# Tokens of a 128-block in another order, longer load runs, sinks over SP: a change to a sliding-window attention and SwiGLU kernel

## The chip, the cores and the metric

The kernel runs on one core of a Trainium2 chip. A core has five engines that run beside each other, each through its own queue in order: TensorE (PE, matrix products and transposes), VectorE (DVE), ScalarE (ACT), GpSimd (POOL) and SyncE (SP). Here POOL and SP mostly issue DMAs; 16 DMA engines do the moving. SBUF is the working memory (128 partitions), PSUM the small memory into which PE writes and which DVE and ACT must empty. The metric is the time of one execution in microseconds; lower is better.

## What is computed

Attention of 4 batches, 8 heads, 768 tokens and head size 64, in which a token sees the 128 latest tokens and the first 4 of its batch (the sinks), then a gated feed-forward block over all 3072 tokens:

```python
scores = scale * np.matmul(q, k.transpose(0, 1, 3, 2))
is_sink = pos[None, :] < int(n_sink)              # 4
rel = pos[:, None] - pos[None, :]
in_window = (rel >= 0) & (rel < int(window))      # 128
scores = np.where(is_sink | in_window, scores, -1000000000.0)
a = softmax(scores); attn = np.matmul(a, v)       # [4, 8, 768, 64]
x = attn.transpose(0, 2, 1, 3).reshape(3072, 512)
g = x @ w_gate                                    # 512 x 1536
out = (g * sigmoid(g)) * (x @ w_val) @ w_out      # [3072, 512]
```

Inputs and output are float32 in HBM; the kernel works in bfloat16 and sums in float32. Loads from POOL's queue convert on the way, so 256 bytes read of a row are 128 bytes written.

## The kernel before

A *group* is 256 tokens (12 groups, 3 per batch), a *block* is 512 tokens of the feed-forward part (6 blocks). Attention of a group runs in steps. **T** (`step_T`): for a pair of heads, four PE transposes turn K and Q into `kqT` (channels on partitions); one copy of 128x512 takes them from PSUM, on ACT, or on DVE for half of them at the start. **S** (`step_S`): scores of a pair of heads into the PSUM tile `s`, ACT takes the exponential into `e`, DVE multiplies by a mask. **K** (`step_K`): scores against the sinks, `es`. **PV** (`step_PV`): per 128 tokens and four heads, nine products of `e` with V (`va`, with a column of ones) and of `es` with the sinks' V (`vsb`); DVE divides. **X** (`step_X`): four transposes give `xT`, the input of the feed-forward block. A block is 12 *gate* units (products `pg` and `pv`, ACT's tanh `th`, DVE's `u` and `ht`) and 4 *down* units (12 products `pd`, ACT's copy `ot`, an output DMA by SP).

The order is written by hand. `later` holds DVE work that is issued a step afterwards (`flush`). First groups 0 and 1 run alone (lines 389 to 394, here called the start); then, in the loop at line 395, the attention steps of the next two groups are put between the two halves of the gates (a table `slots`). DVE's work for a gate frees PSUM: pool `ps_f` has three buffers, and a gate's `pg` is free when `u` is done, its `pv` when `ht` is done. T, K and X share one PSUM buffer (`ps_t`), PV has two (`ps_o`).

All loads stand on POOL's queue in the order of the program: K and Q of groups 0 and 1 with their V, masks, gate weights, group 2, the output weights, group 3, and then the sinks `vc`, 32 DMAs of four rows (line 185). A DMA that POOL issues waits for the one eight before it. The sinks are spread over the heads by one DVE product per batch, `vsb` (line 223), issued in `step_ks` when the batch's first T steps are done. The loads of later groups follow when T of an earlier group is through (line 319).

Of the kernel before, what the change touches and what calls it, by code (L numbers as in the profile page):

```python
# [15 lines left out]
def kernel(  # L16
# [26 lines left out]
    TB = 512  # L43
    NTB = NTOK // TB
    VS = 72
    FG = 3
# [17 lines left out]
    xtp = pool("xtp", 2)  # L64
# [6 lines left out]
    ps_o = pool("ps_o", 2, True)  # L71
    ps_t = pool("ps_t", 1, True)
# [6 lines left out]
    def load_group(g, split=1):  # L79
        b, c = divmod(g, GC)  # L80
        t0 = c * 256
        kq = natp.tile([P, 2, 2, H * D], BF16, tag="kq", name="kq")
        va = vpool.tile([P, 2, H, VS], BF16, tag=f"va{g}", name="va")
        hn = H // split
        for s in range(split):
            hs = slice(s * hn, (s + 1) * hn)
            for i, src in ((0, k), (1, q)):
                for j in range(2):
                    nc.gpsimd.dma_start(  # L89
                        kq[:, i, j, s * hn * D:(s + 1) * hn * D].rearrange(  # L90
                            "p (h d) -> p h d", d=D),
                        src[b, hs, t0 + j * P:t0 + (j + 1) * P].rearrange(
                            "h p d -> p h d"),
                    )
        for j in range(2):
            nc.gpsimd.dma_start(  # L96
                va[:, j, :, 0:D],
                v[b, :, t0 + j * P:t0 + (j + 1) * P].rearrange("h p d -> p h d"),
            )
        nat[g], vas[g] = kq, va  # L100
# [3 lines left out]
    def load_gate(i):  # L104
        n = FG * P
        for lst, w, nm in ((wgs, moe_w_gate, "wg"), (wvs, moe_w_val, "wv")):
            t = wpool.tile([P, DMC, n], BF16, tag=f"{nm}{i}", name=nm)
            nc.gpsimd.dma_start(
                t, w[:, i * n:(i + 1) * n].rearrange("(c p) f -> p c f", p=P))
            lst.append(t)  # L110
# [14 lines left out]
    vcs, vsbs, kss = [], [], []  # L125

    load_group(0, split=2)
    make_identity(nc, ident)


    def build_mask(m, sink):
        nc.gpsimd.memset(m, 1.0)
        for j in range(2):
            pv_, dg = m[:, j, 0:P], m[:, j, P:2 * P]
            nc.gpsimd.affine_select(
                out=pv_, in_=pv_, compare_op=ALU.is_gt, fill=0.0, base=0,
                pattern=[[-1, P]], channel_multiplier=1)
            if sink:
                nc.gpsimd.affine_select(
                    out=pv_, in_=pv_, compare_op=ALU.is_ge, fill=1.0, base=-NS,  # L140
                    pattern=[[0, P]], channel_multiplier=1)
            nc.gpsimd.affine_select(
                out=dg, in_=dg, compare_op=ALU.is_ge, fill=0.0, base=0,
                pattern=[[1, P]], channel_multiplier=-1)
            if sink and j == 0:

                nc.gpsimd.affine_select(
                    out=dg, in_=dg, compare_op=ALU.is_ge, fill=1.0, base=-NS,
                    pattern=[[0, P]], channel_multiplier=1)

    load_group(1)
    build_mask(mask0, True)
    load_gate(0)
    load_gate(1)
    build_mask(mask, False)
    load_gate(2)
    load_gate(3)
    load_group(2)


# [6 lines left out]
        pattern=[[NS, H]], channel_multiplier=-1)  # L167
    KS = P + 2 * NS
    for b in range(B):
        vc = const.tile([P, D + 1], BF16, tag=f"vc{b}", name="vc")  # L170
        nc.vector.memset(vc, 0.0)
        nc.vector.memset(vc[:, D:D + 1], 1.0)
        ks = const.tile([P, NP2 * KS], BF16, tag=f"ks{b}", name="ks")
        nc.vector.memset(ks, 0.0)
        vsb = const.tile([P, H, D + 1], BF16, tag=f"vsb{b}", name="vsb")
        vcs.append(vc)
        kss.append(ks)
        vsbs.append(vsb)

    for i in range(4):  # L180
        load_out(i)
    load_group(3)
    for b in range(B):
        for h in range(H):
            nc.gpsimd.dma_start(vcs[b][h * NS:(h + 1) * NS, 0:D], v[b, h, 0:NS])

    def ones_v(g):
        nc.vector.memset(vas[g][:, :, :, D:D + 1], 1.0)
# [10 lines left out]
    def step_T(g, p, on_dve=False):  # L199
        b, c = divmod(g, GC)  # L200
        if c == 0 and p == 0:
            kqT[b] = kqtp.tile([P, NP2, 2, S], BF16, tag="kqT", name="kqT")
        pt = ps_t.tile([P, 2, 2, P], BF16, tag="pt", name="pt")
        for i in range(2):
            for t in range(2):
                nc.tensor.transpose(  # L206
                    pt[:, i, t], nat[g][:, i, t, p * P:(p + 1) * P], ident)
        dst = kqT[b][:, p, :, c * 256:(c + 1) * 256].rearrange(
            "q i (t r) -> q i t r", t=2)
        if on_dve:  # L210
            nc.vector.tensor_copy(out=dst, in_=pt)  # L211
        else:
            nc.scalar.copy(out=dst, in_=pt)  # L213

    def step_ks(g):

        b = g // GC
        dst = kss[b].rearrange("q (a m) -> q a m", m=KS)
        for h in range(2):
            r = slice(h * D, (h + 1) * D)  # L220
            nc.vector.tensor_copy(
                out=dst[r, :, h * NS:(h + 1) * NS], in_=kqT[b][r, :, 0, 0:NS])
        nc.vector.tensor_tensor(  # L223
# [86 lines left out]
    def T(g, p):  # L310
        def f(pro=False):
            if p == 0:
                ones_v(g)
# [135 lines left out]
```

## Time and profile before

| | us |
|---|---|
| median of 3 runs (327.3 to 330.65) | 330.06 |
| the profiled run / its span | 327.02 / 325.2 |
| start, to the first gate | 0 to 74.4 |
| block 0, with attention of groups 2 and 3 | 74.4 to 117.55 |
| blocks 1 to 4, 43.74, 42.51, 42.99 and 43.75 | to 290.54 |
| block 5, without attention, and the end | to 325.2 |

All numbers are of one profiled execution. Busy times of engines overlap, so they don't add up to the span; what counts is which wait ends last in a stretch. Mean durations of PE rows hold pipelining: products of one kind start closer together than each lasts. Busy over the span: PE 251.2 us, DVE 167.9, ACT 127.2, POOL 95.8. POOL's queue moved 14.18 MB in 81792 packets, most of them under 512 bytes.

### The profile page before, as it was taken

To read this page: it belongs to the slowest core of one execution; us is meant where nothing else is said; L and a number is where in the kernel's file an instruction comes from. 1 tells how busy PE (TensorE), PEld (TensorE's weight loads), DVE (VectorE), ACT (ScalarE), POOL (GpSimd) and SP (SyncE) were. 2 spreads that over 40 slices of the span, in tenths; PEclk is the share of its full clock that TensorE was granted. 3 is DMA by queue.
4 is the path that set the end of the run, shared out by engine and by line. 5 is a ranking of instruction groups with operands and counts; after the bars stand their busy time and mean duration, and the time that the engine had idled before them with its cause. 6 is when DMAs were issued, how large, how long until landed. Compare 5 with 4: busy or idle time off the path is not lost.

```text
span 325.2 us, 4622 instructions
## 1 busy us (share of the span) xinstructions
PE 251.2 (77%) x1824; PEld 128.8 (40%) x1824; DVE 167.9 (52%) x352; ACT 127.2 (39%) x197; POOL 95.8 (29%) x142
## 2 busy tenths in 40 slices
PE   0420000576999988999979999799997999999995
PEld 0210000353454544555434545345453454544442
DVE  2200000663788526886158882378842688617830
ACT  1230000324665136762257541475514666223321
POOL 8996756996532006050042600000000000000000
PEclk9999999999999999999999999999999999999999
DMA  8999999099929129390149932100011000020002
GB/s 56 113 132 203 173 203 90 1 72 124 100 15 84 40 92 73 24 99 30 69 54 78 75 24 90 39 2 3 1 65 67 0 2 0 34 94 3 2 32 97
DMA packets 85268, 20.75 MB, mean 64 GB/s; under 512 B 76544, under 2 KB 82176, under 8 KB 85248
## 3 DMA queue, kind: packets, MB, share of 16 engines
q0 software_dynamic: 81792, 14.18, 55.3%
q1 hardware_dynamic: 3456, 6.29, 5.0%
q8 instruction: 14, 0.23, 0.3%
q14 instruction: 6, 0.05, 0.0%
HBM read 28.34 MB, written 6.29 MB: 107 GB/s over the span
## 4 chain that ended last, share of the span: by engine, by line
PE 63%; DVE 13%; DMA 9%; POOL 7%; ACT 5%; issue 2%; DVEq 0%; POOLq 0%
PE pd L363 18%; PE pv L348 16%; PE pg L340 15%; DVE ht L353 4%; PE o L286 4%; PE s L242 3%; PE pt L206 3%; DMA wg<-in_moe_w_gate_dram 3%; DMA va<-in_v_dram 3%; POOL kq L89 3%; DMA wo<-in_moe_w_out_dram 3%; DVE e L251 2%; DVE u L352 2%; ACT th L343 2%; PE px L304 2%
## 5 line engine op out<-in xcount | busy, mean ns | idle before, releaser
L340 PE MATMUL pg<-xT,wg 128*128 128x512 bf16 x288 | 73.9, 379 | 0.5 <-DVE xT L307 0.5
L348 PE MATMUL pv<-xT,wv 128*128 128x512 bf16 x288 | 74.1, 380 | 0.0
L352 DVE SCALAR_TENSOR_TENSOR u<-th,pg 128x512 bf16<-128x512 f32 x72 | 49.4, 686 | 40.8 <-ACT th L343 39.9
L343 ACT ACTIVATE th<-pg 128x512 f32<-128x512 f32 x72 | 43.0, 597 | 69.4 <-PE pg L340 69.4
L206 PE MATMUL pt<-ident,kq 128*128 128x128 bf16 x192 | 20.2, 233 | 61.2 <-DVE kqT L211 39.9
L363 PE MATMUL pd<-wo,ht 128*128 128x512 bf16 x288 | 65.6, 379 | 0.0
L353 DVE TENSOR_TENSOR ht<-u,pv 128x512 bf16<-128x512 bf16 x72 | 49.5, 688 | 24.1 <-PE pv L348 19.5
L247 ACT ACTIVATE e<-s 128x1024 bf16<-128x1024 f32 (+1 forms) x48 | 45.6, 950 | 9.9 <-PE s L242 9.3
L213 ACT COPY kqT<-pt 128x512 bf16<-128x512 bf16 x44 | 25.8, 585 | 54.6 <-PE pt L206 54.6
L89 POOL DMA_DIRECT2D kq<-in_k_dram x26 | 22.6, 882 | 77.7 <-PE pt L206 76.7
L340 PEld LDWEIGHTS <-wg 128*128 128x128 bf16 x288 | 28.2, 98 | 34.4 <-issue 0.6
L206 PEld LDWEIGHTS <-kq 128*128 128x128 bf16 x192 | 13.6, 103 | 67.6 <-issue 61.2
L363 PEld LDWEIGHTS <-ht 128*128 128x128 bf16 x288 | 27.4, 98 | 30.4
L367 ACT ACTIVATE ot<-pd 128x512 f32<-128x512 f32 x24 | 14.3, 597 | 60.3 <-PE pd L363 60.3
L348 PEld LDWEIGHTS <-wv 128*128 128x128 bf16 x288 | 25.0, 98 | 23.6 <-issue 3.6
L251 DVE TENSOR_TENSOR e<-e,mask 128x1024 bf16<-128x1024 bf16 (+1 forms) x48 | 30.6, 640 | 1.8 <-ACT e L247 1.8
L223 DVE TENSOR_TENSOR vsb<-vc,diag_h 128x520 bf16<-128x520 bf16 x4 | 2.8, 701 | 40.7 <-DMA vc<-in_v_dram 40.6
L89 POOL DMA_DIRECT2D kq<-in_q_dram x26 | 22.6, 885 | 0.8 <-DMA wv<-in_moe_w_val_dram 0.8
L242 PE MATMUL s<-kqT 64*128 64x128 bf16 (+1 forms) x256 | 19.6, 255 | 3.9 <-ACT e L247 3.9
L96 POOL DMA_DIRECT2D va<-in_v_dram x24 | 21.4, 915 | 3.7 <-DMA wo<-in_moe_w_out_dram 1.7
L292 DVE TENSOR_TENSOR xn<-o,rcp 128x256 bf16<-128x256 f32 x48 | 20.4, 425 | 1.7
L286 PEld LDWEIGHTS <-e 128*128 128x128 bf16 x352 | 17.7, 103 | 6.6 <-issue 0.9
(36 smaller groups left out, 126.0 us busy)
## 6 DMA issues: line engine op xcount, KB each, us to landing
out_dram<-ot SPq DMA_DIRECT2D x24, 256.0 KB, 2.0
va<-in_v_dram POOLq DMA_DIRECT2D x24, 128.0 KB, 4.5
kq<-in_k_dram POOLq DMA_DIRECT2D x22, 128.0 KB, 4.2
kq<-in_q_dram POOLq DMA_DIRECT2D x22, 128.0 KB, 4.7
wg<-in_moe_w_gate_dram POOLq DMA_DIRECT2D x4, 384.0 KB, 7.7
wv<-in_moe_w_val_dram POOLq DMA_DIRECT2D x4, 384.0 KB, 8.9
wo<-in_moe_w_out_dram POOLq DMA_DIRECT2D x4, 384.0 KB, 9.1
vc<-in_v_dram POOLq DMA_DIRECT2D x32, 0.5 KB, 1.6
```

Source lines behind the costliest of these rows:

```text
L89: nc.gpsimd.dma_start(kq[:, i, j, s * hn * D:(s + 1) * hn * D].rearrange("p (h d) -> p h d", d=D), src[b, hs, t0 + j * P:t0 + (j + 1) * P] ...
L206: nc.tensor.transpose(pt[:, i, t], nat[g][:, i, t, p * P:(p + 1) * P], ident)
L242: nc.tensor.matmul(ps[:, h, col:col + n], kT[r, kk:kk + P], qT[r, qq:qq + n], start=True, stop=True)
L247: nc.scalar.activation(e, ps[:, :, lo:512], AF.Exp, scale=scale)
L251: nc.vector.tensor_tensor(e, e, m[:, :, lo:512].broadcast_to([P, 2, 512 - lo]), op=ALU.mult)
L286: nc.tensor.matmul(o, l, r, start=(i == 0), stop=(i == len(mms) - 1), skip_group_check=True)
L340: nc.tensor.matmul(pg, wgs[fi][:, c, fs], x[:, c], start=(c == 0), stop=(c == DMC - 1))
L343: nc.scalar.activation(th, pg, AF.Tanh, scale=0.5)
L348: nc.tensor.matmul(pv, wvs[fi][:, c, fs], x[:, c], start=(c == 0), stop=(c == DMC - 1))
L352: nc.vector.scalar_tensor_tensor(u, th, 1.0, pg, op0=ALU.add, op1=ALU.mult)
L353: nc.vector.tensor_tensor(hts[tb][:, f], u, pv, op=ALU.mult)
L363: nc.tensor.matmul(po, hts[tb][:, f, ts * P:(ts + 1) * P], wos[f // n][:, f % n], start=(f == 0), stop=(f == DFC - 1))
```

## The change

Within each block of 128 tokens the tokens are kept in the order (token % 4, token // 4) everywhere: in `kqT`, in the masks, in V's partitions and in the feed-forward input. Only the output write undoes it. This goes with the following parts.

- K and Q are loaded with 4 neighbouring tokens per partition (the first 512 tokens of a batch) or 2 (its last 256), so a run is 4 or 2 rows. `step_T` transposes two tokens of one head at once, and eight copies of 64x256 put them in place, in runs of 32: four on ACT, four on DVE.
- V is loaded by 8 DMAs of 32 partitions per group, where 2 of 128 stood.
- The sinks are loaded as float32 by 8 DMAs on SP's queue at the start, and the four `vsb` products follow at once.
- Masks are built on 32 partitions at a time; the one for a batch's first group is a copy with four rows set to one.
- Blocks are 512, 256, 512, 512, 512, 512 and 256 tokens. After nine gates of block 0, group 2 runs alone; the gates of the 256-token block 1 follow, then the remaining gates of both, then their downs with attention of groups 3 and 4 between.
- PSUM: `ps_o` and `ps_t` become one pool `ps_a` of three buffers. Gate weights come in pieces of 1, 2, 3, 3 and 3 columns of 128. Some SBUF pools change by a buffer.

```diff
-    natp = pool("natp", 4)
+    natp = pool("natp", 2)
-    epool = pool("epool", 3)
+    epool = pool("epool", 2)
-    xtp = pool("xtp", 2)
+    xtp = pool("xtp", 3)
-    ps_o = pool("ps_o", 2, True)
-    ps_t = pool("ps_t", 1, True)
+    ps_a = pool("ps_a", 3, True)
...
+    PARTS = ((0, 4), (512, 2))
+    def load_kq(b, a, k2):
+        t0, r = PARTS[a]
...
+        hs = slice(4 * k2, 4 * k2 + 4)
+        for i, src in ((0, k), (1, q)):
+            nc.gpsimd.dma_start(
+                nat[b, a][:, i, hs],
+                src[b, hs, t0:t0 + r * P].rearrange("h (p r) d -> p h (r d)", r=r))
...
+        nc.vector.memset(va[:, :, :, D:D + 1], 1.0)
         for j in range(2):
-            nc.gpsimd.dma_start(
-                va[:, j, :, 0:D],
-                v[b, :, t0 + j * P:t0 + (j + 1) * P].rearrange("h p d -> p h d"),
-            )
+            t0 = c * 256 + j * P
+            for r in range(4):
+                nc.gpsimd.dma_start(
+                    va[32 * r:32 * (r + 1), j, :, 0:D],
+                    v[b, :, t0 + r:t0 + P:4].rearrange("h m d -> m h d"))
...
+    for h in range(H):
+        nc.sync.dma_start(
+            vcf[h * NS:(h + 1) * NS, :, 0:D],
+            v[:, h, 0:NS].rearrange("b s d -> s b d"))
-        for h in range(H):
-            nc.gpsimd.dma_start(vcs[b][h * NS:(h + 1) * NS, 0:D], v[b, h, 0:NS])
...
+        for h in range(2):
+            for u in range(2):
+                src = pt[u * D:(u + 1) * D, h]
+                dst = kqT[b][h * D:(h + 1) * D, pairs[0]:pairs[-1] + 1]
...
+                    for i in range(2):
+                        evict(h, dst[:, i, :, :, u], src[:, i])
...
+    def evict(h, dst, src):
+        if h == 0:
+            nc.scalar.copy(out=dst, in_=src)
+        else:
+            nc.vector.tensor_copy(out=dst, in_=src)
...
-        nc.sync.dma_start(out[tb * TB + ts * P:tb * TB + (ts + 1) * P], ot)
+        r0 = OFF[tb] + ts * P
+        nc.sync.dma_start(
+            out[r0:r0 + P].rearrange("(m r) d -> r m d", r=4), ot)
...
+    us = ([(gate, 0, f) for f in range(9)] + [(alone, 0, 0)]
+          + [(gate, 1, f) for f in range(9)]
+          + [(gate, tb, f) for f in range(9, 12) for tb in (0, 1)]
+          + [u for u in units(0, 1) if u[0] is down])
```

Three places where instructions move. A row is a line of the program, the operation, the tile written and those read, and the shape; "x8" stands for eight alike. First DVE at the start of the program, before:

```order
L188 MEMSET va 128x16
L211 COPY kqT<-pt 128x2x256 x2
L221 COPY ks<-kqT 64x4x4 x2
L223 TENSOR_TENSOR vsb<-vc,diag_h 128x520
L251 TENSOR_TENSOR e<-e,mask_113 128x2x384 x2
L188 MEMSET va 128x16
L251 TENSOR_TENSOR e<-e,mask_113 128x2x384
L211 COPY kqT<-pt 128x2x256 x2
```

The same place now:

```order
L201 MEMSET ks 128x272 x4
L205 TENSOR_TENSOR vsb<-vcf,diag_h 128x520 x4
L259 COPY kqT<-pt 64x2x4x32 x8
L291 TENSOR_TENSOR e<-e,mask_110 128x2x384
L291 TENSOR_TENSOR e<-e,mask 128x1024
L259 COPY kqT<-pt 64x2x4x32 x4
```

The product `vsb` stood behind the first T steps and ahead of every mask; now all four stand ahead of the first T step's copies.

Second POOL's queue at the start, where it issues loads; before, from the last gate weights to the sinks:

```order
L108 DMA wv<-in_moe_w_val_dram 128x4x384
L89 DMA kq<-in_k_dram 128x8x64 x2
L89 DMA kq<-in_q_dram 128x8x64 x2
L96 DMA va<-in_v_dram 128x8x64 x2
L161 MEMSET diag_h 128x8
L162 AFFINE_SELECT diag_h<-diag_h 128x8
L165 AFFINE_SELECT diag_h<-diag_h 128x8
L117 DMA wo<-in_moe_w_out_dram 128x3x512 x4
L89 DMA kq<-in_k_dram 128x8x64 x2
L89 DMA kq<-in_q_dram 128x8x64 x2
L96 DMA va<-in_v_dram 128x8x64 x2
L185 DMA vc<-in_v_dram 4x64 x32
```

Now, from the masks to the first weights:

```order
L163 AFFINE_SELECT mask<-mask 32x2x128
L167 COPY mask_110<-mask 128x512
L169 MEMSET mask_110 1x256 x4
L105 DMA va<-in_v_dram 32x8x64 x16
L116 DMA wg<-in_moe_w_gate_dram 128x4x128
L116 DMA wv<-in_moe_w_val_dram 128x4x128
L116 DMA wg<-in_moe_w_gate_dram 128x4x256
```

The sinks are gone from this queue, and 16 V loads stand where 4 stood, ahead of the first weights.

Third DVE inside a block with attention (block 2 of the changed kernel); before, in block 0, its gates looked like this:

```order
L251 TENSOR_TENSOR e<-e,mask 128x1024
L188 MEMSET va 128x16
L352 SCALAR_TENSOR_TENSOR u<-th,pg 128x512
L353 TENSOR_TENSOR ht<-u,pv 128x512
L251 TENSOR_TENSOR e<-e,mask 128x1024
```

and now:

```order
L291 TENSOR_TENSOR e<-e,mask 128x1024
L259 COPY kqT<-pt 64x2x4x32 x4
L398 SCALAR_TENSOR_TENSOR u<-th,pg 128x512
L399 TENSOR_TENSOR ht<-u,pv 128x512
L291 TENSOR_TENSOR e<-e,mask 128x1024
```

Four T copies stand ahead of a gate's `u` where none stood.

More of the change, by code (lines that the diff above doesn't have):

```diff
@@ L197, in flush, with step_T @@
         later.clear()
-    def step_T(g, p, on_dve=False):
-        b, c = divmod(g, GC)
-        if c == 0 and p == 0:
+    def step_T(b, a, n):
+        t0, r = PARTS[a]
+        if a == 0 and n == 0:
             kqT[b] = kqtp.tile([P, NP2, 2, S], BF16, tag="kqT", name="kqT")
[L203 to L211, printed above, removed]
-        else:
-            nc.scalar.copy(out=dst, in_=pt)
@@ L393, with alone @@
[L393 to L413 removed]
+    def alone(tb, x, attn):
+        pro(*attn)
+        flush()
```

331 lines of the change are left out of this document (196 added, 135 removed).

## The prediction

> **What bounds the kernel now.** I read the page first: the 40 slices say where TensorE (PE) is empty.
>
> ```profile
> span 325.2 us, 4622 instructions
> ...
> PE   0420000576999988999979999799997999999995
> ```
>
> A slice is 8.1 us. From the second block on PE is at 7 to 9 tenths; in the first nine slices it is nearly empty. Next come the waits (engine and line, what it waited for, total us, times, longest) and the order of time at the start.
>
> ```profile
> DVE vsb L223 <- DMA vc<-in_v_dram: 40.6, 1, 40.6
> PE pt L206 <- DVE kqT L211: 39.9, 2, 39.4
> ```
>
> ```profile
> 1.32 1.65 POOL L89 DMA_DIRECT2D kq<-in_k_dram  x2 [0.81 <-POOLq L430]
> ...
> 4.08 0.10 PEld L206 LDWEIGHTS <-kq 128*128 128x128 bf16 x1 [4.08 <-DMA kq<-in_k_dram]
> ...
> 53.83 12.95 POOL L185 DMA_DIRECT2D vc<-in_v_dram  x26 [0.37 <-DMA va<-in_v_dram]
> 56.14 0.70 DVE L223 TENSOR_TENSOR vsb<-vc,diag_h 128x520 bf16<-128x520 bf16 x1 [40.58 <-DMA vc<-in_v_dram]
> ...
> 61.29 1.02 ACT L247 ACTIVATE e<-s 128x1024 bf16<-128x1024 f32 x1 [1.44 <-PE s L242]
> ...
> 63.01 1.02 ACT L247 ACTIVATE e<-s 128x1024 bf16<-128x1024 f32 x1 [0.70 <-PE s L242]
> ...
> 67.42 0.38 ACT L266 ACTIVATE es<-pk 128x256 bf16<-128x256 f32 x1
> ```
>
> The first vsb product stands in VectorE's (DVE's) queue behind nothing but the sinks, and the sinks were put on POOL's queue behind four groups and all weights. DVE stood 40.6 us, and with it a PSUM eviction (kqT) and all of PE. This is one wait, and it costs the whole 40 us. The stages then go, by windows (from:to, us, busy us of each engine with its count, clock, DMA share, GB/s):
>
> ```profile
> 0.00:74.40 74.40, 16.53 (x153) 11.40 (x153) 15.88 (x50) 11.19 (x14) 61.39 (x103) 1.00 1.25 116
> ...
> 117.55:161.29 43.74, 41.43 (x321) 21.41 (x320) 26.93 (x54) 22.03 (x34) 10.51 (x12) 1.00 0.63 61
> ...
> 290.54:325.20 34.66, 31.08 (x144) 13.92 (x142) 16.51 (x24) 10.15 (x17) 0.00 (x0) 1.00 0.10 38
> ```
>
> ```profile
> 117.55:149.06 31.51, 29.20 (x229) 14.90 (x228) 22.24 (x40) 20.14 (x31) 10.51 (x12) 1.00 0.81 60
> 149.06:161.29 12.23, 12.23 (x94) 6.51 (x92) 4.69 (x14) 1.89 (x4) 0.00 (x0) 1.00 0.18 66
> ```
>
> In a block with attention PE is busy 41.43 of 43.74 us: PE is the bound there, first in twelve gates (31.5 us), then in four downs (12.2). The last block has no attention: 144 matmuls in 31.08 us are 0.216 us each, so a gate (8) is 1.73, a down (12) 2.59, and 34.66 - 31.08 = 3.6 us are the tail.
>
> **The change part by part.** The prices of one instruction (mean ns ahead of the last bar):
>
> ```profile
> L353 DVE TENSOR_TENSOR ht<-u,pv 128x512 bf16<-128x512 bf16 x72 | 49.5, 688 | 24.1 <-PE pv L348 19.5
> ...
> L251 DVE TENSOR_TENSOR e<-e,mask 128x1024 bf16<-128x1024 bf16 x32 | 21.9, 685 | 1.8 <-ACT e L247 1.8
> ...
> L292 DVE TENSOR_TENSOR xn<-o,rcp 128x256 bf16<-128x256 f32 x48 | 20.4, 425 | 1.7
> ...
> L185 POOL DMA_DIRECT2D vc<-in_v_dram x32 | 15.9, 504 | 4.6 <-DMA wo<-in_moe_w_out_dram 2.3 <-DMA kq<-in_k_dram 0.9 <-DMA kq<-in_q_dram 0.9
> ...
> L251 DVE TENSOR_TENSOR e<-e,mask 128x768 bf16<-128x768 bf16 x16 | 8.7, 550 | 0.0
> ...
> L266 ACT ACTIVATE es<-pk 128x256 bf16<-128x256 f32 x8 | 3.1, 384 | 0.0
> ...
> L108 POOL DMA_DIRECT2D wg<-in_moe_w_gate_dram x4 | 3.1, 766 | 0.0
> ...
> L135 POOL TENSOR_SCALAR_AFFINE_SELECT mask<-mask 128x128 bf16<-128x128 bf16 x4 | 1.2, 289 | 0.2
> ```
>
> ```profile
> 126.08 1.03 PE L340 MATMUL pg<-xT,wg 128*128 128x512 bf16 x4
> ...
> 126.41 0.69 DVE L353 TENSOR_TENSOR ht<-u,pv 128x512 bf16<-128x512 bf16 x1
> 127.01 0.69 DVE L251 TENSOR_TENSOR e<-e,mask 128x1024 bf16<-128x1024 bf16 x1
> ...
> 127.37 0.61 PE L261 MATMUL pk<-kqT,ks 128*128 128x256 bf16 x4
> ...
> 127.82 1.03 PE L348 MATMUL pv<-xT,wv 128*128 128x512 bf16 x4
> ```
>
> ```profile
> 133.45 1.03 PE L340 MATMUL pg<-xT,wg 128*128 128x512 bf16 x4
> ...
> 134.67 0.39 PE L206 MATMUL pt<-ident,kq 128*128 128x128 bf16 x4
> 134.89 1.03 PE L348 MATMUL pv<-xT,wv 128*128 128x512 bf16 x4
> ```
>
> Neighbours on DVE start 0.60 us apart though each lasts 0.69: some 0.08 overlaps. The attention steps cost PE what lies between the end of a gate's first half (its start + 4 x 0.216) and the next start: an S step 127.37 - 126.94 = 0.43, the K step (four matmuls of 256 columns) 127.82 - 127.37 = 0.45, a PV step 134.67 - 134.31 = 0.36, four transposes 0.22. So 256 columns cost half of 512.
>
> Sinks: 32 DMAs leave POOL (32 x 0.50 = 16 us of its time, the last of them in front of groups 4 and 5) and 8 go to SP, with nothing before them. An SP issue takes 0.33 us and SP's writes land 2.0 us after issue (next two fences): from about 1.4 us, 8 x 0.33 + 2.0 give 6.1 us. All four vsb products now stand together at the head of DVE (0.70 each, 0.61 apart) and end at 8.7; the first T step's evictions queue behind them.
>
> ```profile
> L368 SPq DMA_DIRECT2D out_dram<-ot x24: 332/332/377, 109.5 to 322.3; - x24
> ```
>
> ```profile
> out_dram<-ot SPq DMA_DIRECT2D x24, 256.0 KB, 2.0
> ...
> vc<-in_v_dram POOLq DMA_DIRECT2D x32, 0.5 KB, 1.6
> kq<-in_k_dram POOLq DMA_DIRECT2D x4, 64.0 KB, 3.0
> ```
>
> ```profile
> 10.00:18.00 8.00, 4.14 (x32) 2.52 (x31) 1.81 (x4) 3.50 (x5) 7.71 (x15) 1.00 1.93 123
> ...
> 26.00:34.00 8.00, 0.00 (x0) 0.00 (x0) 0.00 (x0) 0.00 (x0) 4.94 (x9) 1.00 1.31 203
> ```
>
> K and Q: runs of 128 bytes written go at 123 GB/s (first row, K, Q, V alone), runs of 768 at 203 (weights). The new 512 lie nearer the second. The first 64 KB landed 2.76 us after issue (1.32 to 4.08). A load now has 256 KB, 1.3 us at 203 GB/s, about 1 us more than 64 KB: K of heads 0 to 3 is there near 4.8 and Q, behind it, at 6.1. On POOL stand, from 1.3 us: four issues of 0.76, identity and diagonal 1.2, the masks' 8 selects at 0.29 to 0.4 each (a select of 128 elements is 0.289, these have 256), and a copy and five small memsets, put at 2.5: the masks are done near 11 us, about when the first one is asked for.
>
> V: 96 DMAs of 256 runs for 24 of 1024. An issue is between 0.50 (4 runs) and 0.77 (512 runs); I take 0.65. The 16 of groups 0 and 1 are out at 21.5, landed at 24.5; PV of group 1 asks at 26. Gate chunks follow (2.3 MB at 203 GB/s from 22: 34 us; the fourth is asked at 42), then group 2 (42 us, asked at 47). These loads are thus hidden by the exponentials. The Trainium skill (DMA: Bandwidth & Descriptors, Rules for kernel authors) speaks against this part: under 64 KB a transfer is mostly overhead, so small ones should be joined. Here eight DMAs of 64 KB landed in 3.0 us each but were issued 0.75 apart, so the overhead overlapped; by the rule, paid one after the other, rival 3 follows.
>
> First gate: exponentials start when DVE has evicted its half of the first step, 9.6 us. Eight S steps, four at 1.72 (63.01 - 61.29) and four at 1.5, and 0.7 of evictions that don't fit between: es at 23.5. From es to the first gate took 74.4 - 67.4 = 7.0 before; PV of group 0 adds 1.0. First gate 31.5 instead of 74.4.
>
> T steps: per step 8 transposes as before on PE, but 8 evictions of 64x256, half on ACT, half on DVE, for two of 128x512 on ACT. ACT: es's 0.384 for 256 elements, 0.27 apart. DVE: 145 ns + 0.53 per element (from the two mask rows) gives 0.28 where the source is dense (two thirds), and xn's 0.425 where it steps; both ends are 0.20 (0.28 apart by overlap) and 0.42. Before, DVE evicted almost none of this: in blocks this is new DVE work right ahead of u, which frees a gate's PSUM buffer. What leaves: two T steps per gate on a single PSUM buffer (ps_t), where PE waited for ACT:
>
> ```profile
> PE pt L206 <- ACT kqT L213: 9.4, 10, 0.9
> ```
>
> Stages after, from the prices:
> - Nine gates of block 0, no attention: 15.5, to 47.0.
> - Group 2 alone, PE nearly idle: T 2.8, S 4 x 1.72, es 0.3, PV and X 5.0: 15.0, to 62.0. Before, it lay in gates.
> - Nine gates of 256 columns: PE 0.90, but th 0.38, u 0.42, ht 0.42 and three buffers make 0.97: 8.7, to 70.7.
> - Six gates, half of them 256 wide, with 4 T, 4 S: PE 5.2 + 2.7 for the gates, 4 x 0.44 and 4 x 0.33 for the steps, 11.2 with 0.2 of start; DVE 11.3 (overlapping) to 13.9 (not). Order is tight, since a T's evictions stand ahead of u: 13.5, to 84.2.
> - Six downs 15.5, attention of groups 3 and 4 on PE 5.7 (4 S, 8 PV, K, 4 X; group 3 has no sinks apart), waits 1.8: 23, to 107.2.
> - Block 2, gates: PE 20.7 + 8.9 (6 T at 0.43, 8 S, one K, 5 PV, 2 X) = 29.6; DVE 12 x 1.37, 6 T, 8 masks, 5 PV, 2 X: 28.5 to 33.7. Two engines nearly equal in lockstep: 32.5, and downs 12.2: 44.7. Block 3 in the same way 44.4, block 4 with two T steps 41.7: to 238.0.
> - Blocks 5 and 6: 20.7 + 12 x 0.97 + 6 x 2.59 + 4.6 for group 11: 52.4, to 290.4.
> - Tail 3.6, and the writes below 1.0: 295.0.
>
> Output writes: each names 4 outer runs of 32 rows instead of 128 rows; same bytes, same row size. If they spread as before, +0; if a fourth of the engines carries them, 5.0% of 16 engines' time (next row) is 260 us over 24, 0.68 us on 16, 2.7 on four: +2.0 at the tail, earlier ones hidden by 2.59 per down. No row is nearer to either; I take 1.0.
>
> ```profile
> q1 hardware_dynamic: 3456, 6.29, 5.0%
> ```
>
> The Trainium skill (DMA: Bandwidth & Descriptors, Why a DMA increments its semaphore by 16 and not by 1) says that the number of engines is the largest up to 16 that divides the outermost size of both sides. By it four engines carry these writes and the sum is 1.0 higher; no row of before shows such a write.
>
> Costing nothing: kq's two buffers (its next loads are asked tens of us later), e's two, the smaller weight chunks, memsets of va moved to the start (0.07 each).
>
> The sum, 295.0, is a span; the profiled run took 327.02 for 325.2, so 296.8; the median 330.06 is 0.9% above that run: **299**.
>
> **Rivals.**
> 1. PE stays the bound, DVE's evictions vanish beside it: blocks 2 to 4 -2.9, -2.2, -1.7, mixed gates -2.2, downs -2: 288. For it: DVE is busy 22 of 31.5 us in gates now. Against: it gets a third more there.
> 2. DVE becomes the bound: 0.42 per eviction, no overlap: blocks 2 and 3 +3.8 and +3, mixed gates +2.5, start +1: 309.
> 3. Loads take the place of the sinks (the longer runs bring no speed, or the narrow V loads cost 1.6 each in turn, the sinks' time to land): 16 x 1.6 from 11 us is 36.6 where PV asked at 26, +10.6, and group 2's eight and the gate chunks behind them come some 4 later than asked: about 313. Against: the 0.75 spacing.
> 4. Slower: an eviction with runs of 32 costs DVE far more than its elements. Past 0.42 each tenth of a us adds 18 steps x 4 x 0.1 = 7.2 us; from 309 it passes 333 at 0.75 us. The nearest rows (0.28 to 0.42) are far below.
>
> **How the numbers follow.** Forecast 0.52, rival 1 0.16, rival 2 0.14, rival 3 0.10, rival 4 0.04, and 0.04 between (evictions near 0.7, or loads later still) for 327 to 333. Within 1% is about what a measurement can tell from no change. Faster 0.92, same 0.04, slower 0.04. The range 288 to 313 runs from rival 1 to rival 3; the forecast's own is 291 to 307.
>
> **What would show it.** vsb starting near 6 us; the first pg near 31; a stretch near 47 to 62 us with PE almost empty; kqT rows on DVE of 0.28 and 0.42; DVE's busy share in gates of blocks 2 and 3 near PE's; out writes landing in 2 us or in 4. Wrong if PE waits for va or wg at the start, or if kqT on DVE is over 0.5 us.

## The result, and the profile after

The changed kernel takes 308.47 us (median of 4 runs, 307.91 to 308.69) where the kernel before took 330.16 beside it: a ratio of 0.9357, interval 0.9302 to 0.9412. The forecast was 299, with a range of 288 to 313. The profiled run took 307.91 us for a span of 306.2.

From the page of the changed kernel, the span, PE in 40 slices (7.7 us each) and the granted clock:

```profile
span 306.2 us, 5085 instructions
...
PE   0357896588799988889997897999999999999980
...
PEclk9999999599999999999999799999999999999996
```

Before, PE was at four tenths or less in the first seven slices and at 5 and 7 in the next two; now it is thin in the first four, dips once (slices 7 and 8, group 2 alone), and is empty in the last. The clock row has three dents that the kernel before did not have. Three waits from the list of the changed kernel:

```profile
DVE kqT L259 <- ACT kqT L257: 16.7, 11, 3.1
...
PE pv L394 <- DVE u L398: 8.5, 8, 2.1
...
DVE vsb L205 <- DMA vcf<-in_v_dram: 4.9, 1, 4.9
```

The wait of 40.6 us for the sinks has become one of 4.9. Two new ones stand above it: VectorE's T copies wait for ScalarE's, and PE waits for `u`. The stages, by windows (from:to, us, busy us of PE, PEld, DVE, ACT and POOL with counts, granted clock, DMA share, GB/s; the share is the time that packets took over the time of 16 engines, and can pass 1):

```profile
0.00:33.28 33.28, 15.69 (x153) 10.98 (x153) 20.13 (x64) 13.93 (x26) 29.88 (x56) 1.00 0.85 93
...
48.82:63.90 15.08, 8.27 (x89) 5.78 (x88) 10.37 (x25) 6.97 (x13) 5.53 (x9) 0.66 1.40 192
...
72.53:88.30 15.77, 12.53 (x102) 7.43 (x100) 12.74 (x37) 11.23 (x27) 12.99 (x22) 1.00 1.24 120
...
109.05:155.28 46.23, 41.53 (x314) 21.37 (x312) 33.66 (x79) 23.65 (x49) 19.07 (x31) 1.00 0.66 78
155.28:204.95 49.67, 44.52 (x337) 22.98 (x336) 33.91 (x78) 25.16 (x50) 0.00 (x0) 0.97 0.07 21
204.95:244.23 39.28, 39.03 (x281) 18.95 (x280) 28.90 (x60) 18.93 (x33) 0.00 (x0) 1.00 0.10 28
...
297.20:306.20 9.00, 0.11 (x1) 0.00 (x0) 0.00 (x0) 0.60 (x1) 0.00 (x0) 0.74 0.22 80
```

Block 4, with two T steps, leaves PE idle for 0.25 us of 39.28. Blocks 2 and 3, with six T steps each, leave it idle for 4.7 and 5.2. And from 298 on nothing works but the output writes. These are the largest misses of the forecast, but not the only ones; the stages against the forecast's own:

| stage | forecast | measured |
|---|---|---|
| start, to the first gate | 31.5 | 33.28 |
| nine gates of block 0 | 15.5 | 15.54 |
| group 2 alone | 15.0 | 15.08 |
| nine gates of 256 columns | 8.7 | 8.63 |
| six mixed gates | 13.5 | 15.77 |
| six downs, attention of groups 3 and 4 | 23 | 20.75 |
| block 2 | 44.7 | 46.23 |
| block 3 | 44.4 | 49.67 |
| block 4 | 41.7 | 39.28 |
| blocks 5 and 6 | 52.4 | 52.97 |
| tail | 4.6 | 9.00 |
| span | 295.0 | 306.2 |

### The profile page after: what moved, and what is told of

Same layout as the page of the kernel before. It is cut to its first block, busy times and chain, and to the rows that moved or that the text cites. A ratio compares the mean times of both kernels' runs of the same rounds, so it can differ in the third digit from the quotient of the medians.

```text
span 306.2 us, 5085 instructions
## 1 busy us (share of the span) xinstructions
PE 258.8 (85%) x1920; PEld 140.0 (46%) x1920; DVE 198.2 (65%) x462; ACT 135.6 (44%) x261; POOL 98.4 (32%) x165
## 3 DMA queue, kind: packets, MB, share of 16 engines
q0 software_dynamic: 49888, 14.16, 44.7%
## 4 chain that ended last, share of the span: by engine, by line
PE 65%; DVE 16%; ACT 10%; issue 3%; DMA 1%; SPq 1%; DVEq 0%; ACTq 0%
PE pd L412 20%; PE pv L394 16%; PE pg L386 16%; DVE kqT L259 6%; PE s L282 5%; DVE u L398 4%; ACT e L287 4%; ACT kqT L257 4%; PE o L326 4%; PE pt L233 2%; ACT th L389 2%; PE px L350 2%; DVE ht L399 1%; DMA vcf<-in_v_dram 1%; DVE e L291 1%
## 5 line engine op out<-in xcount | busy, mean ns | idle before, releaser
L394 PE MATMUL pv<-xT,wv 128*128 128x512 bf16 (+1 forms) x336 | 76.8, 351 | 10.4 <-DVE u L398 8.5
L389 ACT ACTIVATE th<-pg 128x512 f32<-128x512 f32 (+1 forms) x84 | 45.1, 536 | 87.6 <-PE pg L386 79.2
L386 PE MATMUL pg<-xT,wg 128*128 128x512 bf16 (+1 forms) x336 | 76.8, 351 | 1.6 <-DVE xT L353 1.0
L398 DVE SCALAR_TENSOR_TENSOR u<-th,pg 128x512 bf16<-128x512 f32 (+1 forms) x84 | 51.2, 610 | 23.7 <-ACT th L389 22.3
L105 POOL DMA_DIRECT2D va<-in_v_dram x96 | 55.8, 619 | 33.1 <-DMA kq<-in_q_dram 11.5
L399 DVE TENSOR_TENSOR ht<-u,pv 128x512 bf16<-128x512 bf16 (+1 forms) x84 | 51.4, 612 | 9.5 <-PE pv L394 1.0
L259 DVE COPY kqT<-pt 64x256 bf16<-64x256 bf16 x96 | 27.9, 330 | 19.7 <-ACT kqT L257 16.7
L291 DVE TENSOR_TENSOR e<-e,mask 128x1024 bf16<-128x1024 bf16 (+1 forms) x48 | 30.8, 642 | 11.0 <-ACT e L287 10.8
L257 ACT COPY kqT<-pt 64x256 bf16<-64x256 bf16 x96 | 30.5, 367 | 15.9 <-PE pt L233 15.4
L282 PEld LDWEIGHTS <-kqT 64*128 64x128 bf16 x256 | 9.4, 100 | 30.5 <-issue 24.1
L326 PE MATMUL o<-va,e 128*128 128x65 bf16 x352 | 20.9, 207 | 0.7 <-DVE xn L332 0.7
```

The lines of the kernel that those rows point to most:

```text
L105: nc.gpsimd.dma_start(va[32 * r:32 * (r + 1), j, :, 0:D], v[b, :, t0 + r:t0 + P:4].rearrange("h m d -> m h d"))
L257: nc.scalar.copy(out=dst, in_=src)
L259: nc.vector.tensor_copy(out=dst, in_=src)
L282: nc.tensor.matmul(ps[:, h, col:col + n], kT[r, kk:kk + P], qT[r, qq:qq + n], start=True, stop=True)
L326: nc.tensor.matmul(o, l, r, start=(i == 0), stop=(i == len(mms) - 1), skip_group_check=True)
L386: nc.tensor.matmul(pg, wgs[fi][:, c, fs], x[:, c, 0:n], start=(c == 0), stop=(c == DMC - 1))
```

## The experiments

Medians of four runs each; the ratio is to the kernel before on the same chip (its medians there were 327.22 to 330.02).

| run | us | ratio and interval |
|---|---|---|
| `b_sp`: before, sinks on SP | 294.48 | 0.8933 (0.8907 to 0.8959) |
| `a_pool`: changed, sinks on POOL as before | 365.42 | 1.1125 (1.1057 to 1.1192) |
| `a_out4`: changed, writes in four DMAs | 302.03 | 0.9172 (0.9127 to 0.9218) |
| `a_twobank`: changed, two PSUM tiles per T | 301.67 | 0.9149 (0.9120 to 0.9177) |
| `a_defer`: changed, DVE's T copies behind `ht` | 299.50 | 0.9094 (0.9055 to 0.9133) |
| `a_defer_out4` | 293.93 | 0.8945 (0.8896 to 0.8995) |
| `a_all3`: that and two PSUM tiles | 297.95 | 0.9082 (0.9033 to 0.9131) |
| `a_weave2`: `a_defer_out4`, group 2 in the gates | 289.06 | 0.8820 (0.8743 to 0.8897) |
| `b_sp_g2`: `b_sp`, group 2 loaded earlier | 296.14 | 0.9002 (0.8955 to 0.9049) |
| `b_sp_g2a`: that and one PSUM pool of three | 285.32 | 0.8683 (0.8643 to 0.8723) |
| `b_g3`: that and group 3 ahead of the down weights | 277.58 | 0.8438 (0.8380 to 0.8495) |
| `b_g3c`: that and ahead of gate chunk 3 | 272.03 | 0.8308 (0.8293 to 0.8323) |

**The sinks alone.** One part of the change is done in the kernel before:

```diff
+    vcf = const.tile([P, B, D + 1], FP32)
+    nc.vector.memset(vcf, 0.0)
+    nc.vector.memset(vcf[:, :, D:D + 1], 1.0)
+    for h in range(H):
+        nc.sync.dma_start(vcf[h * NS:(h + 1) * NS, :, 0:D],
+                          v[:, h, 0:NS].rearrange("b s d -> s b d"))
...
-            nc.gpsimd.dma_start(vcs[b][h * NS:(h + 1) * NS, 0:D], v[b, h, 0:NS])
...
-            vcs[b].rearrange("q (o d) -> q o d", o=1).broadcast_to([P, H, D + 1]),
+            vcf[:, b:b + 1].broadcast_to([P, H, D + 1]),
```

> The kernel before with one part of the change alone: the sinks come as float32 by 8 DMAs on SP's queue at the start, the 32 on POOL are gone, and the diagonal that vsb needs is built beside the identity. Loads, T steps, blocks and writes as before. Theory 1 (the one wait was the whole gain, the other parts cost time together): the first gate comes at 36 us instead of 74.4, the first T of group 2 waits up to 2 us for its loads, all later stages stay: 288 to 292 us, well under the changed kernel's 308.5. Rival (without longer runs the loads take the wait's place): the first gates wait for weights or group 2 until some 50 us: 303 to 312.

Measured: 294.48. The theory holds: this part alone gives 35.5 us, more than the whole change's 21.7. All else in the change costs 14.0 together. It is 2.5 above the range that the theory gave. Two waits of this run:

```profile
PE pt L205 <- ACT kqT L212: 11.1, 13, 0.9
...
PEld L205 <- DMA kq<-in_k_dram: 6.5, 3, 4.1
```

With the sinks out of the way, the loads of group 2 are late, by more than the 2 us that the theory allowed. The wait for the single PSUM buffer of the T steps is not new (11.4 us in the kernel before), but it is now PE's longest in total.

**All but the sinks.** The other way round, the changed kernel gets back 32 DMAs on POOL behind the loads, with each `vsb` product in `step_ks`:

```diff
-        nc.sync.dma_start(
-            vcf[h * NS:(h + 1) * NS, :, 0:D],
-            v[:, h, 0:NS].rearrange("b s d -> s b d"))
...
+    for b in range(B):
+        for h in range(H):
+            nc.gpsimd.dma_start(vcs[b][h * NS:(h + 1) * NS, 0:D], v[b, h, 0:NS])
```

> The changed kernel with its sinks as before: 32 DMAs on POOL behind all the loads of the start, the vsb product of each batch element in VectorE's queue behind that element's ks copies. Theory (the whole gain is the sinks' move, and what the wait costs is set by how much stands ahead of the sinks on POOL): POOL issues its last load of the start at 69.2 us in the changed kernel, against 53.8 before, so vsb of the first element starts near 75.5 instead of 56.1, the first gate near 90, and the run takes 355 to 368 us, slower than the kernel before. Rival (the other parts of the change carry a gain of their own, so that without the sinks' move it still beats the kernel before): under 325.

Measured: 365.42, slower than before, as the theory said. From the order of time of POOL, DVE and PE in this run:

```profile
75.58 15.78 POOL L205 DMA_DIRECT2D vc<-in_v_dram  x32
...
81.08 0.70 DVE L263 TENSOR_TENSOR vsb<-vc,diag_h 128x520 bf16<-128x520 bf16 x1 [60.45 <-DMA vc<-in_v_dram]
...
90.42 1.02 PE L386 MATMUL pg<-xT,wg 128*128 128x512 bf16 x3 [0.52 <-DVE xT L353]
```

More loads stand ahead of the sinks on POOL than before (V in 96 pieces), so DVE waits 60.5 us, and the first gate starts at 90.4. (`vsb` itself started 5.6 us later than expected: the expectation had left out the last four K and Q loads and eight V loads that POOL issues ahead of the sinks.) The same move is worth 35.5 us in one kernel and 57.0 in the other: the price of this wait went with what stood ahead of the sinks in the queue.

**The output writes.** In the changed kernel each write names 4 outer runs of 32 rows. Here it is four DMAs whose outer size is 32:

```diff
-        nc.sync.dma_start(
-            out[r0:r0 + P].rearrange("(m r) d -> r m d", r=4), ot)
+        for r in range(4):
+            nc.sync.dma_start(out[r0 + r:r0 + P:4], ot[32 * r:32 * (r + 1)])
```

> The changed kernel, each output write of 128 rows as four DMAs of 32 rows, one for each outer run. Theory (a write whose outermost size is 4 is carried by 4 of 16 engines, which drain behind the last downs): the end after the last matmul falls from 9.0 us to 4 to 5, 303.5 to 304.5 in all; SP's packets get 16 counters per DMA. Rival (the end is set by SP's longer issue, 0.54 instead of 0.33 us, or by the clock): 307.5 or more, since SP now issues four times as often.

Measured: 302.03, 6.4 less, a little better than expected. The changed kernel's write queue, from its page (packets, MB, share of 16 engines' span), and the DMA share in two windows at its end:

```profile
q1 hardware_dynamic: 3328, 6.32, 6.7%
```

```profile
294.00:297.00 3.00, 3.00 (x16) 1.28 (x14) 0.00 (x0) 0.60 (x1) 0.00 (x0) 1.00 0.26 96
297.00:300.00 3.00, 0.31 (x2) 0.00 (x0) 0.00 (x0) 0.60 (x1) 0.00 (x0) 1.00 0.26 100
```

The share stands at a quarter of the engines, 0.24 to 0.27, from 288 to 303, without a pause between writes. And the packets count the engines: 24 writes of 128 rows and 8 sink loads of 16 rows are 3200; the other 128 are 4 for each of these 32 DMAs. Before, 24 writes with 16 more each made the 3456. The same queue with the write split, and that kernel's end from the last eviction on:

```profile
q1 hardware_dynamic: 4768, 6.33, 8.2%
```

```profile
294.77:299.30 4.53, 0.00 (x0) 0.00 (x0) 0.00 (x0) 0.60 (x1) 0.00 (x0) 1.00 0.31 76
```

4768 is 3200, 16 more for each of 96 writes, and 4 for each of 8 sink loads: 16 engines again. From the last eviction to the end it takes 4.5 us instead of 8.8 (297.40 to 306.2). Those 4.3 us are the write. Of the rest, 1.7 lie in block 3 (47.99 us for 49.67): there the changed kernel has a stretch of half clock that this run lacks (see the last section), and no line of the edit touches it. That part is not a price of the write.

**The two halves of a T step.** In the order of time of the changed kernel, block 3:

```profile
164.66 1.28 ACT L257 COPY kqT<-pt 64x256 bf16<-64x256 bf16 x4
...
165.97 1.53 DVE L259 COPY kqT<-pt 64x256 bf16<-64x256 bf16 x4 [2.29 <-ACT kqT L257]
...
167.51 0.69 DVE L398 SCALAR_TENSOR_TENSOR u<-th,pg 128x512 bf16<-128x512 f32 x1
168.25 1.75 PE L394 MATMUL pv<-xT,wv 128*128 128x512 bf16 x4 [2.07 <-DVE u L398]
```

DVE's four copies start when ACT's four have ended, though they read other columns: both halves lie in one PSUM tile of 2 KB per partition. The gate's `u` stands behind them in DVE's queue, `u` frees the buffer that the next `pv` needs, and PE stands 2.07 us. The Trainium skill (PSUM — Partial Sum Buffer, PSUM bank collisions raise a hardware error) says that two engines must not touch one bank of one 32-partition quadrant at the same time, reads included, and are to be kept apart by a semaphore; the trace agrees, at 16.7 us over eleven steps. Two edits aim at the wait, one by a tile for each half, one by issuing DVE's copies behind the gate's `u` and `ht`:

```diff
-        pt = ps_a.tile([P, 2, 4, P], BF16, tag="a", name="pt")
+        pts = [ps_a.tile([P, 4, P], BF16, tag="a", name="pt") for _ in range(2)]
```

> The changed kernel, the two halves of a T step (ACT's and DVE's) in two PSUM tiles of ps_a instead of one. Theory (DVE's four copies wait until ACT's four are through, because both read one bank; u behind them is late, and pv waits for u): DVE's waits for ACT before kqT, 16.7 us, go; blocks 2 and 3 lose 3 us each, six mixed gates and the two stages alone about 1 each: 299 to 302. Rival 1 (DVE's own work is the bound): the waits move to DVE's neighbours, less than 1.5 us gained. Rival 2 (two of three buffers per T step make PE wait for PSUM): PE pt waits instead, less than 1.5 us gained or a loss.

```diff
         if h == 0:
             nc.scalar.copy(out=dst, in_=src)
+        elif late[0]:
+            later.append(lambda: nc.vector.tensor_copy(out=dst, in_=src))
         else:
...
+            late[0] = fn is not alone
             fn(tb, x, slots.get(i, []))
```

> The changed kernel, DVE's four copies of a T step inside gates and downs issued after ht (through later) instead of ahead of u; still one bank, so they still follow ACT's. Theory (the loss in blocks 2 and 3 is u standing behind copies that wait for ACT): pv's waits on u (8.5 us) go, 301 to 304; the start and group 2 alone stay as they are. Rival (DVE's own work is the bound): same time within 1.5 us, DVE's order makes no difference.

Measured: 301.67, as expected, and 299.50, better than expected. The wait of DVE for ACT is out of the first one's list, and 3.3 us of it are left in the second's. PE's wait for `u` in each:

```profile
PE pv L394 <- DVE u L398: 1.9, 4, 1.0
```

```profile
PE pv L398 <- DVE u L402: 2.5, 3, 1.2
```

8.5 us became 1.9 and 2.5. Blocks 2 and 3 of the run with deferral, by windows:

```profile
107.21:150.32 43.11, 40.64 (x309) 21.19 (x312) 33.88 (x79) 23.68 (x49) 18.76 (x31) 1.00 0.71 84
150.32:195.15 44.83, 42.28 (x332) 22.45 (x336) 33.99 (x78) 25.17 (x50) 0.00 (x0) 1.00 0.08 22
```

DVE does the same work there (33.9 and 34.0 us; 33.7 and 33.9 before the edit), but the blocks are 3.1 and 4.8 us shorter: 8.0 of the 9.0 gained. Some 1.7 of these are the stretch of half clock in block 3, which this run lacks too. So DVE's amount of work was not the bound; its place was.

**Do the two add, and is one cure enough?**

> The changed kernel with two repairs at once: VectorE's four T-step copies issued behind the gate's u and ht, and each output write given as four DMAs of 32 rows. Theory (the two mis-sized terms of the forecast, the halves of a T step in turn and the tail on four DMA engines, are separate costs): they add up, 299.5 less the tail's 4.5 to 6.4 = 293 to 295 us, and the last write lands about 4.7 us after the last eviction begins. Rival (the single repairs gained from the same thing, shorter runs of block 3 in which the clock fell, and not from what they touch): the gains do not add, 297 to 300 us. If the sum is right this also says what all of the change but the sinks' move is worth once repaired: about nothing, since the kernel before with the sinks alone moved ran in 294.5.

Measured: 293.93. 9.0 and 6.4 would make 293.1, or 294.8 if the 1.7 us of half clock, which are missing in both single runs, are counted once. They add. Together they are as much as the 14.0 us that all but the sinks' move had cost: the changed kernel with these two repairs stands where the kernel before stands with its sinks moved (294.48). That does not show that the 14.0 were these two costs, since the other parts can gain and lose as well; what the new token order or the longer runs are worth by themselves no run isolates.

> The run before with, in addition, two PSUM tiles per T step, so that ScalarE and VectorE read different ones. Theory (the deferred copies find ScalarE's long done, so one wait was cured twice): no further gain, within 1.5 us of the run with deferral and split writes, and perhaps a small loss, since a T step takes two of the three shared buffers. Rival (the deferral only hid the wait and the turn still delays what follows): 2 to 5 us faster than that run, 289 to 292.

Measured: 297.95, a loss of 4.0, larger than expected. With two of the three shared buffers taken per T step and DVE's copies issued late, the next T step waits:

```profile
PE pt L233 <- DVE kqT L261: 4.0, 5, 1.5
```

**Group 2 alone.** The stage in which PE is busy 8.27 of 15.08 us is thinned: T, S and K of group 2 go into gates 5 to 8.

```diff
-    add(sl, *((9, a) for a in (*Tb(0), *s2, A(step_K, 2), *v2, *x2)))
+    add(sl, *zip((5, 6), Tb(0)), *zip((6, 7, 7, 8), s2), (8, A(step_K, 2)),
+        *((9, a) for a in (*v2, *x2)))
```

> The changed kernel with deferred copies and split writes (293.9 us), and with group 2's T, S and K steps taken out of the stage that runs alone and put into gates 5 to 8; its PV and X steps stay alone. Theory (the stage of 15.1 us in which TensorE is nearly idle is what keeps the repaired kernel from the 285 of the kernel before with three repairs): the stage shrinks to 5 to 6 us, the gates grow by some 2.5, so 7 less, 286 to 288 us. Rival (group 2's K and Q land only at 42 us, so the gates stand where the stage stood): 291 to 294.

Measured: 289.06, 4.9 less, between the two. In this run:

```profile
54.50:58.80 4.30, 2.91 (x45) 2.04 (x46) 4.05 (x12) 0.00 (x1) 1.73 (x3) 1.00 1.24 206
```

The stage shrank to 4.3 us, no load was waited for, and the clock stayed full; but the nine gates grew by more than the 2.5 expected (the first gate starts at 33.24 and the stage at 54.50, 21.3 us for 15.5). The direction of the theory held, its price for S steps put close together in gates was too low: there PE waited up to 1.27 us for an exponential.

**The kernel before, with repairs.** First, group 2's loads ahead of gate chunks 2 and 3:

```diff
+    load_group(2)
     load_gate(2)
     load_gate(3)
-    load_group(2)
```

> The kernel before with the sinks on SP, and group 2's K, Q and V loaded ahead of gate chunks 2 and 3 instead of behind them. Theory (after the sinks' move the next late thing is that load: TensorE stood 6.5 us for its K and 1.6 us for its Q between 36 and 43 us): 4 to 6 us less than 294.5, so 288.5 to 290.5, and no wait for the gate chunks, which are asked for from about 50 us on. Rival (it only moves the wait to the weights, since the DMA engines are full until about 45 us either way): 293 to 296, with the wait on gate chunk 2.

Measured: 296.14, no gain; the rival was right that the wait only moves, but wrong about where. It went to group 3, whose loads stand behind the down weights (order of time of PE in this run):

```profile
51.97 0.29 PE L205 MATMUL pt<-ident,kq 128*128 128x128 bf16 x1 [3.30 <-DMA kq<-in_k_dram]
...
54.71 1.91 PE L347 MATMUL pv<-xT,wv 128*128 128x512 bf16 x4
```

Then the PSUM pools of the small steps as one, as in the changed kernel:

```diff
-    ps_o = pool("ps_o", 2, True)
-    ps_t = pool("ps_t", 1, True)
+    ps_a = pool("ps_a", 3, True)
```

> The run before with the PSUM of the attention's small steps as one pool of three buffers in place of two and one, as the changed kernel has it. Theory (a T step waits for ScalarE to empty the only buffer, 11.1 us in all): 5 to 9 us less than the run before, 280 to 285 us. Rival (T, K, PV and X steps now queue for the same buffers, and what a deferred VectorE operation holds delays the next T step): within 2 us of the run before.

Measured: 285.32, 10.8 less, 0.3 above the range, though the wait for group 3 grew, since everything ahead of it was sooner. Windows of this run, PE's stand for group 3 and the products behind it:

```profile
43.00:51.45 8.45, 0.35 (x7) 0.12 (x6) 1.25 (x3) 1.51 (x2) 4.21 (x5) 0.82 1.55 192
...
54.30:57.90 3.60, 3.60 (x11) 1.11 (x11) 1.29 (x2) 0.58 (x1) 3.20 (x5) 0.50 2.43 155
```

Now group 3 moves forward, in two steps:

```diff
+    load_group(3)
     for i in range(4):
         load_out(i)
-    load_group(3)
```

> The kernel before with the sinks on SP, group 2 loaded ahead of gate chunks 2 and 3, the PSUM of the small steps as one pool of three buffers (285.3 us), and now group 3 loaded ahead of the down weights too. Theory (the 8.1 us for which TensorE stood at 43 us for group 3's K, with the slower clock behind it, were that load's place behind the down weights): 7 to 9 us less, 276 to 279 us, no such wait left, and the clock at full speed throughout. Rival (the DMA engines are full until about 50 us in any order, so the wait passes to gate chunks 2 and 3 or to the down weights): 283 to 286, with that wait in the list.

```diff
     load_gate(2)
+    load_group(3)
     load_gate(3)
...
-    load_group(3)
     for i in range(4):
```

> The run before (277.6 us) with group 3's loads one place further forward, ahead of gate chunk 3 as well. Theory (TensorE stood 4.1 us in four pieces between 43.7 and 46.9 us for group 3's K and Q, and the two products behind them ran at a lower clock, 1.91 us where 1.03 is usual; both come from that load's place alone): the load comes 0.75 MB, some 3.8 us, earlier, the waits go and the clock stays at full speed, 3 to 5 us less, 272.5 to 274.5. Rival (gate chunk 3, asked for near 53 us, or the down weights, now stand late): 276 to 279 with a wait for one of these.

Measured: 277.58, in the range, though a smaller wait and a stretch at half the clock were left; and 272.03, better than its range. Between these two the step is 5.6 us in medians and some 4.3 by the ratios, since they ran on different chips. The last one's page:

```profile
span 270.3 us, 4555 instructions
...
PE   0457799998999999999999999999999999999994
...
PEclk9999999999999999999999999999999999999999
```

and, in order of time, the place where PE had stood:

```profile
43.12 0.40 PE L204 MATMUL pt<-ident,kq 128*128 128x128 bf16 x4
43.35 1.03 PE L346 MATMUL pv<-xT,wv 128*128 128x512 bf16 x4
```

The T step of group 3 comes without a wait, and the products behind it run at full clock. This kernel, the one before with four moves (sinks to SP, groups 2 and 3 forward in the load order, one PSUM pool), is the fastest of the study: 17% under the kernel before and some 11% under the changed one, by the ratios.

## Why the prediction came out as it did

The time is in the stated range, but past the forecast's own 291 to 307. The stages over the forecast add up to 15.8 us and those under it to 4.7, so part of the agreement is misses that cancel.

**The first cause was right, and more than the whole of the gain.** The prediction put the 40 us on one wait of DVE for the sinks. `b_sp` and `a_pool` show it from both sides: with that part alone 35.5 us are gained, without it the rest loses 35.5. Of the 40 us, 38.2 show at the first gate of `b_sp` (36.22 for 74.40); the late loads of group 2 took part of that back. The vsb product started at 7.85 instead of 6.1, since the last of SP's eight issues was done at 4.0, as put, but its data landed 3.85 us later and not 2.0. The prediction's "first nine slices" nearly empty are seven by the row that it shows.

**The start: 33.28 for 31.5.** K of heads 0 to 3 landed at 5.89 (4.8 forecast), Q at 7.41 (6.1). The four vsb products took 3.24 us instead of 2.6, and DVE's half of the first T step, behind them, was done only at 12.1 instead of 9.6. `es` came at 25.9 instead of 23.5, and the steps from there to the first gate won back 0.6. The masks were done at 13.4 instead of 11, but nothing waited for them. The order of time:

```profile
7.54 0.44 POOL L163 TENSOR_SCALAR_AFFINE_SELECT mask<-mask 32x256 bf16<-32x256 bf16 x1
7.85 3.24 DVE L205 TENSOR_TENSOR vsb<-vcf,diag_h 128x520 bf16<-128x520 f32 x4 [4.94 <-DMA vcf<-in_v_dram]
8.03 0.83 POOL L160 TENSOR_SCALAR_AFFINE_SELECT mask<-mask 32x256 bf16<-32x256 bf16 x1
```

**Nine gates, group 2 alone, nine gates of 256 columns** came out within 0.1 us each. Their prices were rows of the trace before. For group 2 alone it was luck in part: up to its first PV step it took 10.7 us for 10.0, since its first scores stood 1.35 us for DVE's copies, and PV and X took 4.3 for 5.0.

**The T steps: the prices were right, the placing failed.** A copy on DVE was put between 0.28 and 0.42 and measured 0.330 in the mean. But the prediction counted DVE's half as work alone (its "Two engines nearly equal in lockstep" are PE and DVE) and put no wait of DVE for ACT in the sum, and DVE's half comes after ACT's. The stages with T steps came out 2.3 (mixed gates), 1.5 (block 2) and 5.3 us (block 3, some 1.7 of it the stretch of half clock) over the forecast; deferral, which leaves the work as it is, gained 9.0. The order of the changed kernel showed the four copies ahead of `u` on DVE; that they read the tile that ACT was reading was there to be seen in `step_T`.

```profile
L259 DVE COPY kqT<-pt 64x256 bf16<-64x256 bf16 x96 | 27.9, 330 | 19.7 <-ACT kqT L257 16.7
...
L257 ACT COPY kqT<-pt 64x256 bf16<-64x256 bf16 x96 | 30.5, 367 | 15.9 <-PE pt L233 15.4
```

**The writes: the term of the sum that was mis-sized.** 1.0 us was put, between 0 and 2.0; the tail came out 4.4 longer. The step that failed is "earlier ones hidden by 2.59 per down". 6.7% of 16 engines' time over the span is 328 us, 13.7 per write, so 3.4 on four engines, where 2.7 was put: longer than a down. Six downs follow each other at the end, each write starts later than its down ends, and the backlog of the earlier ones lands in the tail: the last eviction ended at 298.0, but the rows of the last write moved from 301.9 to 304.9. The Trainium skill's rule on the number of engines (DMA: Bandwidth & Descriptors, Why a DMA increments its semaphore by 16 and not by 1), which the prediction weighed against the trace, holds here by the packet counts; the sum that it gave there was still 3.4 too low, for want of the backlog.

**Block 4 and the downs with attention of groups 3 and 4 were put too high,** by 2.4 and 2.3 us: PE was busy there throughout, and waits that the prediction allowed did not occur. These two hid part of the two misses.

**The rivals.** The first (DVE's copies vanish, 288) did not occur in the changed kernel. The second gave 309, which is nearly the time measured, but by luck and not for its reason: DVE's copies cost 0.330 and not 0.42, and DVE's work was no bound, as the deferral shows. The third (loads take the sinks' place): V's 32 KB loads landed 2.6 us after issue in the median, and no PV step waited for one. (The list puts 1.1 us of a gate's `pv` down to a V load; that product reads no V, and it started at 75.99, when `u` of the gate before had ended at 75.93.) The fourth needed 0.75 us per copy.

**From span to time.** 1.8 us outside the span came as forecast (1.7 in the profiled run). The 0.9% between profiled run and median was particular to the runs before; here it was 0.2%. (296.8 and 0.9% are 299.5, which the prediction wrote as 299.)

**Loads.** The longer runs do what the prediction said: POOL's queue used 55.3% of 16 engines' 325.2 us before and 44.7% of 306.2 after, 180 us and 137. What that bought no run isolates; the fastest kernel of the study has the short runs, and its wait for group 3 went by the order of the loads alone.

## What to carry to other kernels

When one wait explains a gap, price the move that ends it alone, and every other part of the change alone too: here one small part was worth 35 us and the rest lost 14. Work that is split over two engines is not parallel just because it is split: here the halves read one PSUM tile and ran in turn, and with two tiles the wait was gone. And a copy in front of the instruction that frees a buffer can cost more than its duration. After a wait is gone, look again for the load that is late next and move it forward in the queue before its work is asked for; three such moves and a shared PSUM pool were worth some 21 us beyond the first.

## What the runs showed of the hardware

**The clock after PE stands.** After 8.45 us in which PE did 0.35 us of work, the granted clock was 0.50, and four products took 1.91 us where 1.03 is usual (`b_sp_g2a`). The Trainium skill (TensorE: Matmul & The Clock Gate, What's actually happening) puts the fall to half the clock after an idle window of some 3.4 us; the windows with 0.50 agree with the half. In the changed kernel a stand of 2.07 us, with PE fully busy in the two microseconds ahead of it, was followed by a `pv` of 1.75. That is shorter than the skill's figure, and yet:

```profile
168.00:172.00 4.00, 3.75 (x17) 1.55 (x17) 3.29 (x7) 0.25 (x1) 0.00 (x0) 0.57 0.00 0
```

In `a_out4` the same stand at the same place left the clock full:

```profile
167.32 1.02 PE L394 MATMUL pv<-xT,wv 128*128 128x512 bf16 x4 [2.07 <-DVE u L398]
```

So a stand of 2 us can cost the clock and need not; what decides it these runs do not show. Here it made block 3 differ by 1.7 us between two kernels with the same products there.

The clock's row does not show all of it: in the kernel before, after PE's stand of 39 us, four transposes took 0.58 us where 0.39 is usual, and four `pk` products 1.04 where 0.61 is usual, while the column read 1.00 (order of time, and two windows):

```profile
58.65 0.58 PE L206 MATMUL pt<-ident,kq 128*128 128x128 bf16 x4 [39.43 <-DVE kqT L211]
...
66.35 1.04 PE L261 MATMUL pk<-kqT,ks 128*128 128x256 bf16 x4
```

```profile
56.00:66.00 10.00, 4.97 (x54) 3.45 (x55) 6.49 (x17) 3.66 (x4) 10.00 (x21) 1.00 0.05 3
66.00:74.40 8.40, 6.17 (x63) 4.55 (x59) 5.78 (x17) 1.35 (x2) 8.40 (x11) 1.00 1.42 90
```

The trace of that run holds its first clock record, a change to full, at 72.9 us, and the column reads 1.00 where there is no record. The transposes ahead of the stand took 0.58 as well (at 9.81), so PE was slow there from the start; in the changed kernel the first record stands at 31.9.

So durations of like rows are the surer sign. A late load can thus cost more than its wait: the last move gained 4.3 to 5.6 us where the waits in its place were 2.9.

**POOL's selects beside DVE.** The first four of the eight mask selects took 0.44 us each, the last four 0.80 to 0.89 while DVE ran the four vsb products. In `a_pool`, where DVE runs no such product at that time (only T copies, from 9.16 on), all eight took 0.44 or 0.45:

```profile
9.35 0.45 POOL L156 TENSOR_SCALAR_AFFINE_SELECT mask<-mask 32x256 bf16<-32x256 bf16 x1
```

The Trainium skill (GPSIMD Engine Reference, Specifications) says that GpSimd shares its SBUF interfaces with VectorE and contends with instructions that have two SBUF inputs, which the vsb product has; these two runs agree. It goes both ways: in `b_sp`, with no select beside it, each vsb product of this form took 0.70 us, and here up to 0.93, which is why the four took longer than forecast.
